# Dense products allowed beside the attention one round sooner

## The chip, the cores and the metric

The kernel runs on one core of a Trainium2 chip. The metric is the device time of one execution in microseconds (us). Three runs of the kernel before took 573.58, 574.50 and 574.53 us, with a median of 574.5 us.

## The reference

Three stages follow one another on 1536 tokens (2 batches of 768) with 512 features, all in float32:

```python
# attention: 8 heads of 64, causal window of 96 keys and 8 global keys, linear bias by distance
scores = scale * q @ k.T + bias            # masked outside the window and the global keys
x = softmax(scores) @ v                    # heads side by side: x is 1536 x 512
# first block: three products, elementwise maximum, one product
x = maximum(maximum(x @ w1, x @ w2), x @ w3) @ w_out          # 512 -> 768 -> 512
# second block: root mean square norm, gate and value, one product
xn = x / sqrt(mean(x * x) + 1e-6) * rms_g
out = (silu(xn @ w_gate) * (xn @ w_val)) @ w_out              # 512 -> 1536 -> 512
```

The weights and keys arrive as 64-bit floats, and the kernel converts the weights itself.

## The kernel before, in words

**Rounds of attention.** `FastAttention.steps` walks over 24 pieces of attention: 6 chunks of 256 tokens times 4 pairs of heads. It is a software pipeline over rounds, counted by `r` in `fast`, from 0 to 27. Round r does the scores of piece r (TensorE, L785), their maximum with bias on VectorE (L798) and their exponentials on ScalarE (L802), for the two blocks i = 0 and 1 of the chunk. In the same round it divides the piece r - 1 by its sums (`normalise`: two small VectorE operations at L810 and L811, then four GpSimd operations at L816), transposes piece r - 2 (L826, copied out at L833 and L835), multiplies piece r - 3 with the values (L849) and writes its result as a high part (ScalarE, L862). The low part of piece r - 4 is written by VectorE at L860, among the first operations of the round. The generator stops three times in a round: after the first block of exponentials (part 0), after the value products (part 1), and at the end (part 2).

**Dense products beside it.** In parts 0 and 1 of a round, `fast` may issue half a dense product of the first block: `next(side)` advances `early()`, which goes through `first(f, c)` for f = 0, 1 and the token groups c = 0, 1, 2 of 384 tokens. A dense product is 12 matmuls (L379): 4 slices of 128 features times 3 combinations of high and low parts, and its first matmul takes the low part of the weights. Its first half reads the features of the pairs 0 and 1, its second half those of the pairs 2 and 3. Six products (12 halves) make one group, so a group takes 6 rounds at two halves a round. A result is taken out of PSUM one product later, by ScalarE (L394) for the first of three weights and by VectorE (L396) for the other two. Group c may begin at the round that the condition in `fast` names: 12, 16 and 24 for c = 0, 1, 2. As each group takes 6 rounds, the groups run in the rounds 12 to 17, 18 to 23 and 24 to 27, and the last four halves of group 2 come after the attention, ahead of all other dense products, in one unbroken stretch of TensorE work.

**Weights.** `Weights.run` is a generator that converts one unit (128 x 512 weights) after another in small steps, in a cycle of four steps a unit once the ring is in use. One cycle for the unit u: a step without work; a step in which VectorE masks bits of unit u + 1 (L143) and ScalarE casts the high part of unit u (L165); a step with the second bit operation of unit u + 1 (VectorE, L145) and the scaling of unit u + 2 (ScalarE, L137); and a step with the third bit operation of unit u + 1 (VectorE, L151), the fetch of unit u + 3 and the low part of unit u (GpSimd, L168). Only then is unit u done. The steps are pushed in two ways. `pace(n)` makes n steps at the end of a round: 1 from round 1, 2 from round 8, 3 from round 12. And `need`, called by `first` ahead of each product, makes as many steps on the spot as the unit still lacks:

```python
    def need(self, key):
        while key not in self.done:
            next(self.run)
```

In group 0 a round uses one unit: the units 0 to 5 are those of (f, w) = (0, 0) to (1, 2).

**Order.** Up to the end of the attention the order of instructions on TensorE, VectorE, ScalarE and GpSimd is the order of this program (`manual(FRONT)`); the queue of DMAs on SyncE is ordered by a planner. After the attention only TensorE's order is written out, and the planner places the rest.

Of the kernel before, what the change touches and what calls it, by code (L numbers as in the profile page):

```python
# [26 lines left out]
NPAIR = H // 2  # L27
# [7 lines left out]
CN = CB * P  # L35
KC = NPREV + CB * (NG + P)
C2 = 384
NC2 = NT // C2
# [12 lines left out]
LEAD = 3  # L51
# [936 lines left out]
def program(ctx, tc, io):  # L988
# [33 lines left out]
    ngf, nlf = full[:, 0:1], full[:, 1:2]  # L1022

    fast(tc, io, (ident, gcol, mhalf), nlf, ngf)
    rv = nc.values_load(cni[0:1, 0:1], min_val=0, max_val=4)
    with tc.If(rv < 4):
# [3 lines left out]
def fast(tc, io, consts, nlf, ngf):  # L1030
    chunks = [(b, c) for b in range(B) for c in range(NCH)]

    def manual(engines):
        return tc.manual_schedule(engines={getattr(mybir.EngineType, e) for e in engines})

    with ExitStack() as ctx:
        body = Body(tc, ctx, io, consts)
        w = body.weights

        def early():  # L1040


            for c in range(NC2 - 1):
                yield from body.firsts(0, 2, c, c + 1)

        with ExitStack() as c2:
            body.warm_up(c2)
            with manual(FRONT):
                att = FastAttention(body, c2, Masks(tc, c2, nlf, ngf), chunks)
                side, n_side, r = early(), 0, 0  # L1050
                for part in att.steps():
                    if part < 2:

                        c = n_side // 12
                        if r < WARMR:
                            body.keep_warm(r)
                        if c < NC2 - 1 and r >= LEAD + 1 + NPAIR * -(-(c + 1) * C2 // CN):
                            next(side)
                            n_side += 1
                    else:  # L1060
                        if r >= WROUND:
                            w.pace(1 + (r >= WMORE) + (r >= WMOST))
                        r += 1
        body.open_behind()
        with manual(BEHIND):
            for n, _ in enumerate(side):
                w.pace(n % 2)
            for n, _ in enumerate(body.firsts(0, 2, NC2 - 1, NC2)):
                w.pace(n % 2)
            body.behind()  # L1070
            with manual(FRONT):
                body.gated()
# [77 lines left out]
```

## Time and profile before

| what | value |
| --- | --- |
| median of 3 runs | 574.5 us |
| the profiled execution | 575.12 us |
| its span, first to last instruction | 573.3 us |
| TensorE (PE) busy | 561.1 us, 98% of the span |
| VectorE (DVE) busy | 380.2 us, 66% |
| ScalarE (ACT) busy | 251.1 us, 44% |
| GpSimd (POOL) busy | 241.5 us, 42% |
| mean granted TensorE clock | 0.992 |

The profiled execution took 575.12 us, 1.82 us more than its span and 0.62 us more than the median of the runs. Busy time is an average over stages. The chain of work that ended last lies on PE for 93% of the span, so PE's order and PE's waits set the time; in the attention rounds the other engines are busy too, and what matters there is which of them is late for PE.

### The profile page before, as it was taken

To read this page: it belongs to the slowest core of one execution; us is meant where nothing else is said; L and a number is where in the kernel's file an instruction comes from. 1 tells how busy PE (TensorE), PEld (TensorE's weight loads), DVE (VectorE), ACT (ScalarE), POOL (GpSimd) and SP (SyncE) were. 2 spreads that over 40 slices of the span, in tenths; PEclk is the share of its full clock that TensorE was granted. 3 is DMA by queue.
4 is the path that set the end of the run, shared out by engine and by line. 5 is a ranking of instruction groups with operands and counts; after the bars stand their busy time and mean duration, and the time that the engine had idled before them with its cause. 6 is when DMAs were issued, how large, how long until landed. Compare 5 with 4: busy or idle time off the path is not lost.

```text
span 573.3 us, 9229 instructions
## 1 busy us (share of the span) xinstructions
PE 561.1 (98%) x3316; PEld 508.4 (89%) x3316; DVE 380.2 (66%) x801; ACT 251.1 (44%) x606; POOL 241.5 (42%) x301
## 2 busy tenths in 40 slices
PE   6999999999999999999999999999999999999995
PEld 3777888899999999988899999999999998888884
DVE  5899889628679512166778788888887879852220
ACT  3888776514244101166755444444443436442210
POOL 4555564406155001057646666555655616420000
PEclk8899999999999999999999999999999999999999
DMA  8567663202535300000000222222222104303001
GB/s 296 186 197 241 215 213 93 94 1 74 160 99 183 111 1 0 1 1 1 1 0 1 73 75 74 75 73 74 74 74 74 44 31 148 110 3 128 35 22 42
DMA packets 15895, 48.73 MB, mean 85 GB/s; under 512 B 2016, under 2 KB 2016, under 8 KB 15840
## 3 DMA queue, kind: packets, MB, share of 16 engines
q1 hardware_dynamic: 15840, 48.05, 25.9%
q8 instruction: 28, 0.46, 0.3%
q14 instruction: 27, 0.22, 0.1%
HBM read 44.90 MB, written 3.15 MB: 84 GB/s over the span
## 4 chain that ended last, share of the span: by engine, by line
PE 93%; DVE 3%; ACT 1%; POOL 1%; DMA 1%; issue 1%; SPq 0%; DVEq 0%; ACTq 0%
PE q L500 28%; PE mm L379 27%; PE acc L584 17%; PE mo L426 8%; PE sc L785 4%; PE tr L826 4%; PE av L849 4%; PE tr L460 1%; DMA ni<-nn 1%; DVE s L798 1%; PE idle L369 0%; POOL op L254 0%; ACT xb L464 0%; ACT s L802 0%; DVE z L481 0%
## 5 line engine op out<-in xcount | busy, mean ns | idle before, releaser
L500 PE MATMUL q<-xb,op 128*128 128x384 f32 x1008 | 175.5, 334 | 0.5 <-POOL op L254 0.5
L500 PEld LDWEIGHTS q<-xb,op 128*128 128x128 f32 x1008 | 174.6, 188 | 0.8 <-POOL op L254 0.8
L379 PE MATMUL mm<-xt,w 128*128 128x384 f32 x864 | 157.8, 338 | 0.0
L379 PEld LDWEIGHTS mm<-xt,w 128*128 128x128 f32 x864 | 148.4, 188 | 3.0 <-issue 2.6
L168 POOL TENSOR_TENSOR w<-x,w 128x512 fp32r<-128x512 f32 x36 | 51.8, 1442 | 82.8 <-ACT w L165 82.8
L254 POOL TENSOR_TENSOR op<-s,op 128x256 fp32r<-128x256 f32 x48 | 36.2, 766 | 57.5 <-ACT op L253 57.5
L816 POOL TENSOR_SCALAR s<-s,rs 128x232 f32<-128x232 f32 (+1 forms) x96 | 43.3, 471 | 37.0 <-DVE rs L811 27.8
L396 DVE TENSOR_TENSOR h<-mm,h 128x384 f32<-128x384 f32 x48 | 26.5, 553 | 45.8 <-PE mm L379 45.6
L426 PE MATMUL mo<-w,rst 128*128 128x512 f32 x216 | 52.1, 395 | 0.0
L802 ACT ACTIVATE s<-s,nmx 128x232 f32<-128x232 f32 (+1 forms) x96 | 44.5, 467 | 11.9 <-DVE nmx L798 11.6
L584 PE MATMUL acc<-w,gst 128*128 128x512 f32 x216 | 49.2, 389 | 0.0
L584 PE MATMUL acc<-w,st 128*128 128x512 f32 x216 | 49.1, 389 | 0.0
L584 PEld LDWEIGHTS acc<-w,st 128*128 128x128 f32 x216 | 40.5, 188 | 8.4
L584 PEld LDWEIGHTS acc<-w,gst 128*128 128x128 f32 x216 | 40.5, 188 | 8.4
L426 PEld LDWEIGHTS mo<-w,rst 128*128 128x128 f32 x216 | 39.8, 188 | 8.0
L517 DVE TENSOR_TENSOR h<-q,h 128x768 f32<-128x768 f32 (+1 forms) x39 | 34.7, 891 | 3.9 <-PE q L500 3.4
L253 ACT CAST op<-s 128x256 fp32r<-128x256 f32 x48 | 18.1, 401 | 42.2 <-DVE s L234 29.5
L798 DVE CUSTOM_DVE_ANT_0 s<-sc,bias 128x232 f32<-128x232 f32 (+1 forms) x96 | 32.0, 376 | 6.5 <-PE sc L785 4.9
L520 ACT ACTIVATE g<-g 128x768 f32<-128x768 f32 (+1 forms) x26 | 20.8, 799 | 34.0 <-DVE g L517 34.0
L165 ACT CAST w<-x 128x512 fp32r<-128x512 f32 x36 | 22.2, 619 | 26.3 <-DVE x L151 18.0
L785 PE MATMUL sc<-qk 64*128 64x232 f32 (+1 forms) x192 | 28.0, 387 | 4.2 <-DVE nmx L798 2.8
L517 DVE TENSOR_TENSOR g<-q,h 128x768 f32<-128x768 f32 (+1 forms) x13 | 11.6, 895 | 26.9 <-PE q L500 26.9
(104 smaller groups left out, 740.1 us busy)
## 6 DMA issues: line engine op xcount, KB each, us to landing
raw<-wgv SPq DMA_DIRECT2D x24, 512.0 KB, 3.6
raw<-w SPq DMA_DIRECT2D x18, 512.0 KB, 3.9
raw<-wo SPq DMA_DIRECT2D x18, 512.0 KB, 3.7
qk<-qk SPq DMA_DIRECT2D x24, 312.0 KB, 4.2
v<-vwin SPq DMA_DIRECT2D x10, 512.0 KB, 5.6
out<-o SPq DMA_DIRECT2D x12, 256.0 KB, 2.1
v<-vwin SPq DMA_DIRECT2D x2, 256.0 KB, 5.4
gcol<-gcol SPq DMA_DIRECT2D x1, 2.0 KB, 1.6
```

Of the source, the lines that this page charges most:

```text
L168: self.nc.gpsimd.tensor_tensor(out=t[:, 1, :], in0=self.x.pop(i), in1=t[:, 0, :], op=ALU.subtract)
L254: nc.gpsimd.tensor_tensor(out=t[:, 1, :], in0=s, in1=t[:, 0, :], op=ALU.subtract)
L379: self.nc.tensor.matmul(ps, w[:, wi, k * P:(k + 1) * P], x[b][:, k, xi, c0:c0 + C2], start=(i == 0), stop=(i == 3 * KT - 1),)
L396: self.nc.vector.tensor_tensor(out=h, in0=ps, in1=h, op=ALU.max)
L426: self.nc.tensor.matmul(ps, h[:, k % 3, hi, :], w[:, wi, :], start=(k + x == 0), stop=(k == NF1 - 1 and x == 2),)
L500: nc.tensor.matmul(ps, a[:, wi, k * P:(k + 1) * P], self.xb[b][:, j, k, xi, :], start=(i == 0), stop=(i == 5))
L517: nc.vector.tensor_tensor(out=o, in0=ps, in1=x, op=ALU.add)
L584: self.nc.tensor.matmul(ps, of(si), w[:, wi, :], start=(f == LAST[0] and si == 1), stop=(f == LAST[-1] and si == 0 and wi == 0),)
L785: nc.tensor.matmul(sc[j][:, i, :n], qk[r, i * P:(i + 1) * P], qk[r, k0:k0 + n], start=True, stop=True)
L798: nc.vector.tensor_tensor_reduce(out=s[:, j, :n], in0=self.sc[d][j][:, i, :n], in1=self.bias(n, 2 * pr + j), scale=-QK, scalar=3.0e38, op0 ...
L802: nc.scalar.activation(s[:, j, :n], s[:, j, :n], AF.Exp, bias=nmx[:, j:j + 1], scale=-1.0, accum_out=sm[:, i, j:j + 1])
L816: nc.gpsimd.tensor_scalar(s[:, j, :n], s[:, j, :n], rs[:, i, j:j + 1], 1.0, op0=ALU.mult, op1=ALU.mult)
```

## The change

The constant in the condition is one smaller. Group c may begin at the rounds 11, 15 and 23 in place of 12, 16 and 24. Nothing else differs; the steps of `pace` stay tied to the round's number.

```diff
                         c = n_side // 12
                         if r < WARMR:
                             body.keep_warm(r)
-                        if c < NC2 - 1 and r >= LEAD + 1 + NPAIR * -(-(c + 1) * C2 // CN):
+                        if c < NC2 - 1 and r >= LEAD + NPAIR * -(-(c + 1) * C2 // CN):
                             next(side)
                             n_side += 1
```

## Rows read from the trace of the kernel before

**Rows 1.** Page, part 1: busy time, share of the span and instructions of each engine.

```profile
PE 561.1 (98%) x3316; PEld 508.4 (89%) x3316; DVE 380.2 (66%) x801; ACT 251.1 (44%) x606; POOL 241.5 (42%) x301
```

**Rows 2.** Page, part 5: busy us, mean ns | idle us before.

```profile
L379 PE MATMUL mm<-xt,w 128*128 128x384 f32 x864 | 157.8, 338 | 0.0
```

**Rows 3.** Windows by round, 11 to 16: length, busy us by engine, clock, DMA.

```profile
42.40:45.94 3.54, 3.42 (x33) 2.69 (x33) 3.47 (x15) 3.54 (x12) 1.77 (x5) 1.00 0.86 315
45.94:51.42 5.48, 5.48 (x45) 4.49 (x45) 5.41 (x18) 4.58 (x20) 3.65 (x7) 1.00 0.72 235
51.42:56.58 5.16, 5.16 (x46) 4.19 (x45) 5.06 (x16) 3.80 (x13) 3.26 (x5) 1.00 0.71 228
56.58:61.52 4.94, 4.94 (x43) 3.98 (x42) 4.70 (x19) 4.37 (x14) 2.84 (x5) 1.00 0.39 86
61.52:66.25 4.73, 4.73 (x40) 3.76 (x39) 3.86 (x16) 3.04 (x11) 2.85 (x5) 1.00 0.90 334
66.25:71.14 4.89, 4.89 (x39) 3.92 (x38) 3.96 (x15) 3.38 (x13) 1.59 (x4) 1.00 0.70 219
```

**Rows 4.** Chain in order of time, after the attention: start us, us, what.

```profile
118.68 67.80 PE mm L379 x390
```

**Rows 5.** Timeline of PE, rounds 11 to 16: start us, us, what.

```profile
43.70 1.09 PE L826 MATMUL tr<-ident,s 128*128 128x128 f32 x8
44.72 1.10 PE L849 MATMUL av<-at,v 104*64 104x128 f32 x16
...
47.07 1.09 PE L826 MATMUL tr<-ident,s 128*128 128x128 f32 x8
...
49.14 1.10 PE L849 MATMUL av<-at,v 104*64 104x128 f32 x16
50.17 1.31 PE L379 MATMUL mm<-xt,w 128*128 128x384 f32 x6
...
58.02 1.30 PE L379 MATMUL mm<-xt,w 128*128 128x384 f32 x6
...
62.97 1.29 PE L379 MATMUL mm<-xt,w 128*128 128x384 f32 x6
...
67.86 1.29 PE L379 MATMUL mm<-xt,w 128*128 128x384 f32 x6
```

**Rows 6.** Timeline of POOL, rounds 12 to 21.

```profile
51.89 1.66 POOL L168 TENSOR_TENSOR w<-x,w 128x512 fp32r<-128x512 f32 x1 [1.27 <-ACT w L165]
...
57.31 1.59 POOL L816 TENSOR_SCALAR s<-s,rs 128x128 f32<-128x128 f32 x4 [1.73 <-ACT w L165]
58.87 1.28 POOL L168 TENSOR_TENSOR w<-x,w 128x512 fp32r<-128x512 f32 x1
...
71.27 1.28 POOL L168 TENSOR_TENSOR w<-x,w 128x512 fp32r<-128x512 f32 x1 [3.21 <-ACT w L165]
...
93.50 3.20 POOL L816 TENSOR_SCALAR s<-s,rs 128x232 f32<-128x232 f32 x4 [0.44 <-PE tr L826]
```

**Rows 7.** Timeline of DVE, rounds 12 to 14, and one row of round 21.

```profile
51.72 0.69 DVE L151 SCALAR_TENSOR_TENSOR x<-raw,x 128x512 int32<-128x512 int32 x1
...
55.68 0.42 DVE L143 TENSOR_SCALAR x<-x 128x512 int32<-128x512 int32 x1
...
56.74 0.17 DVE L810 TENSOR_SCALAR rs<-sm 128x4 f32<-128x4 f32 x1
...
57.60 0.29 DVE L798 CUSTOM_DVE_ANT_0 s<-sc,bias 128x128 f32<-128x128 f32 x1 [0.17 <-PE sc L785]
...
58.03 0.55 DVE L396 TENSOR_TENSOR h<-mm,h 128x384 f32<-128x384 f32 x1
...
59.13 0.69 DVE L835 COPY at<-tr 128x512 f32<-128x512 f32 x1
59.73 0.97 DVE L151 SCALAR_TENSOR_TENSOR x<-raw,x 128x512 int32<-128x512 int32 x1
...
93.53 0.95 DVE L143 TENSOR_SCALAR x<-x 128x512 int32<-128x512 int32 x2
```

## The prediction

> **What bounds the kernel now.** I read the page first: PE is busy for 561.1 us, 98% of the span [rows 1], and of the 864 dense matmuls of the first block none had idle time ahead of it [rows 2]. So only two things can change the time: work taken off PE's queue where it is the bound, or a new wait on PE. Next the windows, one for each round [rows 3]: a round with two dense halves lasts 4.73 to 5.48 us and PE is busy throughout; round 11, the last without them, lasts 3.54 us, and there VectorE (3.47) and ScalarE (3.54) are as full as PE (3.42). The chain of waits shows what comes after the attention: one piece of 390 dense matmuls in 67.80 us without a gap [rows 4], 0.174 us each. Last the timelines of PE, GpSimd and VectorE around rounds 11 to 16 [rows 5 to 7], for how early each weight unit is ready.
>
> **The move on PE.** Every group slides by one round: group 0 to rounds 11 to 16, group 1 to 17 to 22, group 2 to 23 to 27. Rounds 12 to 27 keep two halves each, round 11 gains two, and two halves leave the stretch after the attention.
>
> What leaves: 12 x 0.174 = 2.09 us.
>
> What round 11 gains: between transposes and values the first half adds (49.14 - 47.07) - (44.72 - 43.70) = 1.05 us; values take 50.17 - 49.14 = 1.03; from the second half to the next round's scores it is 51.42 - 50.17 = 1.25 [rows 3, 5]. Values of round 11 began at 44.72, so round 12 begins at 44.72 + 1.05 + 1.03 + 1.25 = 48.05 in place of 45.94. Round 12 no longer waits for VectorE to clear the scores, so it costs what round 13 does, 5.16 in place of 5.48. Round 13 begins at 53.21 in place of 51.42: 1.79 later. The move alone is worth 1.79 - 2.09 = -0.30 us: round 11 was already nearly full, so little was free there.
>
> The inputs of round 11 cost nothing: its first half reads pieces 0, 1, 4, 5, finished two rounds before; its second half needs piece 7's low part, which VectorE writes at the round's start, ahead of that round's maxima, and PE comes to it only after transposes, a half and values (3.1 us). If that cover failed it would cost up to the 0.4 us of one such operation. The evacuations move with their products; VectorE's round 12 chain stays short enough, since its first result goes to ScalarE.
>
> **The weights.** Counting steps in the code, unit u is done with step 10 + 4u. By the end of round 10 `pace` has made 13 steps, by the ends of rounds 11 to 15 it has made 15, 18, 21, then 25 and 29 once a forced step is added in each of rounds 14 and 15. Unit u is now needed in round 11 + u. Units 0 to 2 (steps 10, 14, 18) are done in time; units 3, 4, 5 (22, 26, 30) each lack exactly one step, so `need` makes it on the spot in rounds 14, 15, 16. That step holds GpSimd's low part, which the product's first matmul reads, and an L151 on VectorE between the two blocks' maxima. Before, 12 + u left each unit done at the end of the previous round; even so unit 5's low part ended at 71.27 + 1.28 = 72.55 in round 17, which began at 71.14 and came to its dense half some 1.6 us later: 0.2 us to spare [rows 3, 5, 6].
>
> Forced or not, GpSimd takes that operation after the round's normalise (57.31, then 58.87 in round 14 [rows 6]), as before. Now PE waits for it, and behind the waiting matmul stand the values, the second half and the next scores. The wait comes out of these durations [rows 6, 7]: VectorE's first maximum 1.02 us after the round's start (57.60 - 56.58); block 0 of the maxima 0.43; evacuation and block 1 1.10 (0.55 without the evacuation); copy 0.60; L143 and L145 1.06; from the division's start to the normalise 0.57; normalise 1.56; low part 1.28. PE comes to its dense half 1.44, 1.45 and 1.61 us after the start of rounds 14, 15 and 16.
>
> Round 14, begun at 53.21 + 5.16 = 58.37: round 13's chain is 53.21 + 1.02 + 0.43 + 1.10 + 0.60 + 1.06 = 57.42 for the division, 57.99 normalise, 59.55 low part, ready at 60.83. Wanted at 59.81: PE waits **1.02**.
>
> Round 15, begun at 58.37 + 4.94 + 1.02 = 64.33: round 14's maxima of block 0 end at 59.82; the forced L151 comes while the low part runs. When that happened before, L151 took 0.97 and ended 0.55 after the low part [rows 6, 7]; so it ends at 61.38; + 1.10 + 0.60 + 1.06 = 64.14 for the division, normalise 64.71 to 66.27, ready 67.55. Wanted 65.78: PE waits **1.77**.
>
> Round 16, begun at 64.33 + 4.73 + 1.77 = 70.83: round 15's L151 begins at 65.78 and takes its undisturbed 0.69 [rows 7]; + 0.55 + 0.60 + 1.06 = 68.68, normalise 69.25 to 70.81, ready 72.09. Wanted 72.44: **no wait**; the earlier wait gave the other engines time.
>
> Sum: -0.30 + 1.02 + 1.77 = +2.49 us. Bounds: if L151 never waited for GpSimd, round 15's wait is 0.90 and round 16's 0.52, in all -0.30 + 1.02 + 0.90 + 0.52 = +2.14. If round 15's L151 waits too, to 67.55 + 0.55, round 16 waits 1.28: +3.77. If the low parts were ready, -0.30. I take +2.49, from the rows nearest to it. Unit 2 ended at 51.89 + 1.66 = 53.55 [rows 6] and is wanted near 54.65 in round 13: no wait, and 1 us of slack if ScalarE's cast slips behind the later values.
>
> Row 58.87 with row 59.73 shows that L151 and the low part exclude each other. A normalise took 3.20 us beside two L143 [rows 6, 7], against 1.59 (smaller tiles) in round 14, so it takes part too. The Trainium skill (SBUF — State Buffer, section "SBUF: two separate sides") states it as an exclusive lock: a VectorE operation with two SBUF inputs or in a two-port mode and a GpSimd operation block each other for a whole instruction. By it round 15's L151 and the normalise would push each other, the low part would be ready at about 68.24, the wait there 2.46 and none in round 16: an estimate of +3.18 us in place of +2.49.
>
> Rounds 17 on need no new weights until after the attention, and PE is their bound, so the 2.49 us are not won back. The profiled execution would take 575.12 + 2.5 = 577.6; its 0.62 us over the median are its own, so the median goes from 574.5 to **577.0**.
>
> **Rivals.**
> *No wait, not slower:* the low parts of units 3 to 5 come before PE does, at the dense half's place in rounds 14 to 16. Then only the move is left, 574.2. It decides at 1 us: the normalise of round 14 would have to start at 56.97 in place of 57.99. For it: no dense matmul waited before [rows 2]. Against: the normalise hangs on the division behind the previous round's maxima, and PE's round 14 is not later relative to those than before.
> *The waits repeat:* L151 loses to GpSimd in rounds 14 and 15 and PE waits in all three rounds, +3.8, 578.3. For it: the 0.97 and the 3.20. By the lock as the skill states it the waits would be longer without repeating; its 577.7 lies between this and the forecast and shares this chance. Against: after each long wait the next round's chain starts from a late PE, which takes from its wait.
> *The planner's part:* after the attention VectorE and ScalarE work is placed anew, and VectorE already runs later units' L143 in round 21 [rows 7]. If these moves freed or delayed PE by 1 us, the time would be 576 or 578; PE's 67.80 us without a gap [rows 4] speak against it.
> That the change does nothing is out: r = 11 satisfies the new condition.
>
> **Chances.** The forecast with the bounds around it 0.60, repeated waits 0.15, no wait 0.15, a planner's move 0.10. From no change this kernel can be told at about 0.2%, 1.15 us. The forecast and repeated waits are slower, with a little of the forecast's low side and half of the planner's case within the bound: slower 0.76; no wait falls mostly within it: same 0.18; faster 0.06. The range reaches from the no-wait case's edge, 574.4, to 579.0, repeated waits with 0.7 more.
>
> **What would show it.** Dense matmuls from round 11, at about 45 us. In the list of waits a new row of PE's L379 waiting for POOL's L168, two or three times, some 2 to 4 us in all; L151 once or twice near 1.5 us in these rounds. Round 13 begins near 53.2, the last values near 118.7 + 1.8 + 2.8 = 123, and the unbroken stretch after them is 2.1 us shorter. Wrong if L379 waits for nothing, or if the wait sits at another place.

## The result, and the profile after

The changed kernel took 577.88 us (median of 4 runs, 576.88 to 578.92) against 574.11 us for the kernel before (573.58 to 574.53): a ratio of 1.0063, 95% interval 1.0048 to 1.0079. It is slower by 3.8 us. The forecast was slower by 2.5 us. Here and below the ratio and its interval come from the undisturbed runs alone (two of the twelve of experiment 3 were disturbed, at 620 and 1115 us). The ratio is not the quotient of the two medians; the two can differ by 0.001.

The profiled execution took 576.88 us, its span 575.0 us. The list of PE's waits has one row that the kernel before did not have, the second one here (the kernel before had no idle time ahead of any L379 [rows 2]). Columns: engine and line, what it waited for, us in total, times, longest us.

```profile
PE sc L785 <- DVE nmx L798: 3.1, 5, 1.1
PE mm L379 <- POOL w L168: 2.8, 2, 2.0
```

The windows by round answer to [rows 3]: the rounds 11 to 16, each from the start of its scores to the start of the next. The columns are the length; the busy us (and instructions) of PE, of its weight loads, of VectorE, ScalarE and GpSimd; the granted clock; the DMA share and GB/s.

```profile
41.43:47.08 5.65, 5.65 (x45) 4.66 (x45) 5.58 (x18) 5.32 (x19) 3.65 (x7) 1.00 0.90 322
47.08:52.24 5.16, 5.16 (x45) 4.20 (x44) 4.93 (x19) 3.60 (x13) 1.82 (x5) 1.00 0.61 177
52.24:57.40 5.16, 5.16 (x45) 4.20 (x44) 3.83 (x16) 3.86 (x13) 3.15 (x7) 1.00 0.54 165
57.40:63.42 6.02, 5.22 (x44) 4.02 (x43) 4.92 (x16) 3.66 (x13) 2.44 (x5) 1.00 0.53 139
63.42:70.36 6.94, 4.99 (x40) 3.79 (x39) 4.66 (x17) 3.93 (x14) 5.11 (x10) 1.00 0.79 276
70.36:75.25 4.89, 4.89 (x39) 3.93 (x39) 3.77 (x13) 3.31 (x12) 1.11 (x1) 1.00 0.39 116
```

Round 11 now holds two dense halves and lasts 5.65 us. Round 14 lasts 6.02 us in place of 4.94, round 15 6.94 in place of 4.73, and in just these two PE is busy for less than the round. Round 16 lasts what it lasted. PE's timeline shows where the holes are; the bracket is the idle time ahead of the row and what ended it. They answer to the dense halves of [rows 5].

```profile
43.58 1.29 PE L379 MATMUL mm<-xt,w 128*128 128x384 f32 x6
...
59.90 1.32 PE L379 MATMUL mm<-xt,w 128*128 128x384 f32 x6 [0.80 <-POOL w L168]
...
67.06 1.31 PE L379 MATMUL mm<-xt,w 128*128 128x384 f32 x6 [1.95 <-POOL w L168]
```

The brackets count from the end that the profile models for the transposes. Counted by starts, the dense halves begin 59.90 - 57.40 = 2.50 and 67.06 - 63.42 = 3.64 us after the start of their rounds, in place of 1.44 and 1.45: 1.06 and 2.19 us later, nearly all that the two rounds grew by.

The timelines of GpSimd and of VectorE in the rounds 14 and 15 answer to [rows 6, 7].

```profile
57.03 1.58 POOL L816 TENSOR_SCALAR s<-s,rs 128x128 f32<-128x128 f32 x4 [2.01 <-DVE rs L811]
58.58 1.26 POOL L168 TENSOR_TENSOR w<-x,w 128x512 fp32r<-128x512 f32 x1
63.64 2.13 POOL L816 TENSOR_SCALAR s<-s,rs 128x128 f32<-128x128 f32 x4 [3.80 <-DVE rs L811]
65.74 1.26 POOL L168 TENSOR_TENSOR w<-x,w 128x512 fp32r<-128x512 f32 x1
```

```profile
58.86 1.53 DVE L151 SCALAR_TENSOR_TENSOR x<-raw,x 128x512 int32<-128x512 int32 x1
...
63.07 0.16 DVE L810 TENSOR_SCALAR rs<-sm 128x4 f32<-128x4 f32 x1
...
64.76 0.69 DVE L151 SCALAR_TENSOR_TENSOR x<-raw,x 128x512 int32<-128x512 int32 x1
```

The low part ends at 59.84 and at 67.00, and each time PE's dense half begins 0.06 us later. The chain in order of time gives the start of the unbroken dense stretch after the attention, [rows 4]:

```profile
122.73 77.33 PE mm L379 x445
```

Up to round 11 both kernels run the same program, and its length differs from execution to execution: between 12 and 20 us the granted clock was 0.50 and then 0.72 (4 us each) in the profile of before, 0.59 and then 1.00 in this one. So I count from the start of round 11's scores: 122.73 - 41.43 = 81.30 us to the stretch, where it was 118.68 - 42.40 = 76.28. From the stretch's start to the end of the span it is 575.0 - 122.73 = 452.27 in place of 573.3 - 118.68 = 454.62. So the trace accounts for 5.02 - 2.35 = +2.67 us, while the medians differ by 3.77. That gap of 1.1 us was the open question for the experiments.

### The profile page after: what moved, and what is told of

It reads as the page before. It is cut to its first block, busy times and chain, and to the rows that moved or that the text cites. A ratio compares the mean times of both kernels' runs of the same rounds, so it can differ in the third digit from the quotient of the medians.

```text
span 575.0 us, 9225 instructions
## 1 busy us (share of the span) xinstructions
PE 560.1 (97%) x3316; PEld 507.5 (88%) x3316; DVE 380.4 (66%) x801; ACT 251.4 (44%) x606; POOL 240.1 (42%) x301
## 3 DMA queue, kind: packets, MB, share of 16 engines
HBM read 44.90 MB, written 3.15 MB: 84 GB/s over the span
## 4 chain that ended last, share of the span: by engine, by line
PE 92%; DVE 4%; POOL 1%; issue 1%; DMA 1%; ACT 1%; SPq 0%; DVEq 0%; ACTq 0%; POOLq 0%
PE q L500 28%; PE mm L379 26%; PE acc L584 17%; PE mo L426 8%; PE sc L785 4%; PE tr L826 4%; PE av L849 4%; PE tr L460 1%; DVE s L798 1%; DMA qk<-qk 1%; PE idle L369 0%; POOL op L254 0%; ACT xb L464 0%; POOL s L816 0%; DVE z L481 0%
## 5 line engine op out<-in xcount | busy, mean ns | idle before, releaser
L379 PE MATMUL mm<-xt,w 128*128 128x384 f32 x864 | 158.1, 338 | 2.8 <-POOL w L168 2.8
L379 PEld LDWEIGHTS mm<-xt,w 128*128 128x128 f32 x864 | 148.4, 188 | 6.0 <-POOL w L168 3.2
```

What stands on the lines that cost most here:

```text
L379: self.nc.tensor.matmul(ps, w[:, wi, k * P:(k + 1) * P], x[b][:, k, xi, c0:c0 + C2], start=(i == 0), stop=(i == 3 * KT - 1),)
```

## The experiments

Ratios are to the kernel before, run beside each kernel on the same chip (573.72 us in the first four experiments, 573.78 us in the next four).

**1. The changed kernel again.**

> The changed kernel itself, once more, beside the kernel before. Theory (PE waits for the low parts of the weight units 3 to 5): again two or three waits of PE's dense matmuls (L379) for GpSimd's L168 in rounds 14 to 16, lengthening these rounds by 3.0 to 3.6 us in all; from the start of round 11's scores to the start of the unbroken dense stretch 81.0 to 81.6 us against 76.3 before; ratio to before 1.004 to 1.006. Rival (most of the loss comes from outside these rounds, since the timed runs differ by 3.8 us and the profiles from round 11 on by only 2.7): a ratio of 1.006 or more with waits of 3.3 us, and in the profile a second place, later than round 16, that is over 1 us slower than before.

577.91 us, ratio 1.0068 (1.0049 to 1.0087). The waits were as before, 2.6 us in two, but 123.77 - 41.09 = 82.68 us passed from round 11 to the stretch, 1.4 more than in the first profile. All of it lies in round 15, which lasted 71.44 - 63.09 = 8.35 us. PE's timeline there:

```profile
66.61 1.64 PE L379 MATMUL mm<-xt,w 128*128 128x384 f32 x6 [1.82 <-POOL w L168]
68.17 1.55 PE L849 MATMUL av<-at,v 128*64 128x128 f32 x12
69.65 1.85 PE L379 MATMUL mm<-xt,w 128*128 128x384 f32 x6
71.44 1.05 PE L785 MATMUL sc<-qk 64*128 64x232 f32 x8
```

The same 12 value matmuls take 0.88 us in other rounds. The windows show what differs (the number after the engines' busy times is the granted TensorE clock):

```profile
66.61:67.30 0.69, 0.69 (x4) 0.69 (x5) 0.66 (x3) 0.29 (x2) 0.00 (x0) 1.00 0.82 260
67.30:70.90 3.60, 3.60 (x20) 2.83 (x19) 1.11 (x4) 1.13 (x3) 1.74 (x5) 0.53 0.51 198
70.90:71.44 0.54, 0.54 (x4) 0.29 (x3) 0.00 (x0) 0.33 (x1) 0.54 (x1) 1.00 0.00 0
```

In the 3.6 us from 0.69 us after the second wait on, the granted clock was 0.53 in the mean, about the lower of its two levels, 1.2 and 2.4 GHz. In the first profile it was 1.00 there. Neither theory nor rival had this: the second loss is in the same round as the wait, not later.

**2. Conversion sooner, from the early rounds.**

```diff
-WMORE = 8
+WMORE = 5
```

> The changed kernel with the second conversion step a round from round 5 on in place of round 8 (WMORE = 5): three steps earlier, so that no unit needs a forced step. Theory: the dense waits for L168 fall from 3.3 us to under 0.4 us, the rounds 14, 15, 16 last 4.9, 4.7 and 4.9 us, and the time is 0.3 us (up to 0.6) below the kernel before, ratio 0.9985 to 1.0005, if the three added steps hide in rounds 5 to 7; each that does not costs up to 0.7 us. Rival (the loss is the planner's or the moved halves' own, not the weights'): still 1.004 or more.

576.61 us, ratio 1.0046 (1.0030 to 1.0061). No dense matmul waited for GpSimd any more, and from round 11 to the stretch it was 122.44 - 44.33 = 78.11 us, 3.2 less than in the first profile of the changed kernel. The waits are gone as the theory said, yet the time is where the rival put it, and the reason is a third one: the three added steps did not hide. The rounds 4 to 10 took 24.97 us:

```profile
19.36:44.33 24.97, 22.66 (x220) 17.14 (x219) 23.58 (x92) 20.93 (x74) 13.98 (x29) 1.00 0.53 167
```

Before, they took 42.40 - 19.65 = 22.75 us, with VectorE busy for 20.79 of them, 91%; now it is 23.58 us, 94%. In these rounds PE's scores waited 2.3 us for VectorE, against 0.6 before. Over the whole execution it is 4.6 us, against 2.8:

```profile
PE sc L785 <- DVE nmx L798: 4.6, 6, 1.3
```

The three added steps cost 24.97 - 22.75 = 2.22 us, about the 0.7 us a step that I had named as the most. The medians differ by 2.9 us; the rest is not placed.

**3. The low part of the weights last in each product.**

```diff
-        for k in range(KT):
-            for wi, xi in ((1, 0), (0, 1), (0, 0)):
+        order = [(k, 0, xi) for k in range(KT) for xi in (1, 0)] + [(k, 1, 0) for k in range(KT)]
+        for k, wi, xi in order:
...
-            if k == KT // 2 - 1:
+            if i == 6:
                 yield
```

> The changed kernel with another order in each dense product: the eight matmuls with the high part of the weights first, the four with the low part last, so that the first half needs no low part. The forced steps stay where they are. Theory (PE's wait for the low part is the loss): the wait moves to the last two thirds of the second half, some 2.8 us later, and vanishes but for 0.3 us; ratio 0.9985 to 1.001. Rival (the forced step's VectorE work between the maxima is the loss, by making the next scores late): rounds 14 and 15 stay 1 us or more longer than before, ratio 1.003 or more.

Ratio 1.0010 (0.9995 to 1.0024). The forced steps are still there; only PE's need for the low part comes later. Round 14 lasts 63.36 - 58.41 = 4.95 us, as before the change; round 15 lasts 5.55, with one wait inside the second half:

```profile
68.02 0.96 PE L379 MATMUL mm<-xt,w 128*128 128x384 f32 x4 [0.55 <-POOL w L168]
```

The theory holds in place and kind; I had expected at most 0.3 us to be left and 0.55 was. In round 14, which also has a forced L151 between the maxima (59.87 to 61.44), PE lost nothing, so that work by itself does not delay PE in its round.

**4. The kernel before with late weights.** No dense product is moved.

```diff
-WMORE = 8
-WMOST = 12
+WMORE = 10
+WMOST = 13
```

> The kernel before, dense products from round 12 as there, but conversion made one round later (WMORE = 10, WMOST = 13), so that the units 3, 4 and 5 are forced in rounds 15, 16 and 17 just as the changed kernel forces them in 14, 15 and 16. Theory (the weights alone are the loss): waits of L379 for L168 of 2 to 3.6 us in these rounds, and with 0.3 us less VectorE work ahead of round 12 a ratio of 1.003 to 1.006, as for the changed kernel. Rival (it takes the earlier dense products to make the loss): within 0.002 of the kernel before.

577.87 us, ratio 1.0071 (1.0050 to 1.0093): a loss as large as the changed kernel's, without the change. One row of the list of waits, and two windows of the round with the second wait:

```profile
PE mm L379 <- POOL w L168: 2.9, 2, 1.9
```

```profile
65.91:69.60 3.69, 1.86 (x15) 1.32 (x14) 3.13 (x13) 2.58 (x10) 3.25 (x5) 1.00 0.35 101
...
70.90:74.48 3.58, 3.58 (x20) 2.81 (x19) 0.60 (x2) 1.46 (x3) 2.90 (x5) 0.53 0.11 42
```

The ratio is above the 1.006 that I gave for the waits alone, and the fall of the clock is here too: 0.53 behind a wait of 1.89 us.

**5. The forced steps made one round end earlier.**

```diff
-                            w.pace(1 + (r >= WMORE) + (r >= WMOST))
+                            w.pace(1 + (r >= WMORE) + (r >= WMOST) + (13 <= r <= 15))
```

> The changed kernel with one conversion step more at the end of each of rounds 13, 14 and 15 (four in place of three), so that the steps that were forced inside the next rounds are made at the end of the rounds before, ahead of the next normalise on GpSimd. Theory (only the lateness of the low parts costs): L379's waits for L168 fall to under 0.4 us, no fall of the granted clock after round 11, 78.0 to 78.6 us from round 11's scores to the unbroken dense stretch (82.7 in the first experiment, 76.3 before), ratio to before 0.999 to 1.001. Rival (the same number of steps in rounds 13 to 15 loads VectorE as much as the forced steps did, and the scores become late instead): ratio 1.003 or more, with waits of the scores for VectorE in rounds 14 to 17.

573.72 us, ratio 1.0005 (0.9995 to 1.0015): in three rounds one step is made at the end of the round before and not inside the round, and the loss is gone. The rounds 13 to 16 make 15 steps as in the changed kernel, the forced ones counted, so the amount of VectorE's work was not the cause. GpSimd now does the low part ahead of the normalise:

```profile
56.97 1.27 POOL L168 TENSOR_TENSOR w<-x,w 128x512 fp32r<-128x512 f32 x1 [2.23 <-ACT w L165]
58.21 1.58 POOL L816 TENSOR_SCALAR s<-s,rs 128x128 f32<-128x128 f32 x4
61.91 1.36 POOL L168 TENSOR_TENSOR w<-x,w 128x512 fp32r<-128x512 f32 x1 [2.12 <-ACT w L165]
63.71 1.58 POOL L816 TENSOR_SCALAR s<-s,rs 128x128 f32<-128x128 f32 x4 [0.44 <-DVE rs L811]
```

In round 14 (57.12 to 62.06) the low part is ready at 58.24, where in the changed kernel PE waited for it until 2.5 us into the round. The rounds 14 and 15 last 4.94 and 4.73 us, the clock stays at 1.00, and 119.34 - 41.15 = 78.19 us pass to the stretch.

```profile
57.12:62.06 4.94, 4.94 (x43) 3.98 (x42) 4.32 (x15) 3.54 (x13) 2.82 (x6) 1.00 0.72 193
62.06:66.79 4.73, 4.73 (x39) 3.76 (x38) 4.63 (x16) 3.43 (x13) 2.80 (x5) 1.00 0.86 298
```

**6. Experiments 3 and 5 together.**

> The extra step at the end of rounds 13 to 15 and the product order with the low part of the weights last, together on the changed kernel. Theory: no wait of a dense matmul for GpSimd at all, so that what is left is the move alone: 78.0 to 78.2 us from round 11's scores to the unbroken stretch, ratio 0.999 to 1.000. Rival (half of the measured gain of the product order came from something else): ratio 1.001 or more.

573.76 us, ratio 0.9997 (0.9986 to 1.0008), 120.39 - 42.29 = 78.10 us to the stretch and 572.5 - 120.39 = 452.11 behind its start, no wait for GpSimd. This is the move alone, and by its time it cannot be told from no change.

**7. Control: the product order of experiment 3 on the kernel before.**

> Control: the kernel before with the product order that has the low part of the weights last. Theory: no dense matmul waited before, so nothing changes, ratio 0.999 to 1.001, and 76.2 to 76.4 us from round 11's scores to the unbroken stretch. Rival (the order itself slows or speeds the products): the stretch after the attention differs by more than 0.5 us.

573.70 us, ratio 1.0000 (0.9990 to 1.0010), 118.29 - 41.98 = 76.31 us to the stretch and 572.4 - 118.29 = 454.11 us behind its start. The order by itself does nothing, so what it gave in experiment 3 came from the wait. The traces of experiments 6 and 7 have the same product order and no wait, and differ by the move alone: 78.10 - 76.31 = 1.79 us more up to the stretch and 454.11 - 452.11 = 2.00 less behind its start, -0.21 in all.

**8. Both dense halves behind the values.**

```diff
                     if part < 2:
-                        c = n_side // 12
                         if r < WARMR:
                             body.keep_warm(r)
-                        if c < NC2 - 1 and r >= LEAD + NPAIR * -(-(c + 1) * C2 // CN):
-                            next(side)
-                            n_side += 1
+                        for _ in range(2 * part):
+                            c = n_side // 12
+                            if c < NC2 - 1 and r >= LEAD + NPAIR * -(-(c + 1) * C2 // CN):
+                                next(side)
+                                n_side += 1
```

> The changed kernel with both dense halves of a round after the value products in place of one on either side of them; the forced steps come after the copy then. PE reaches the first low part 1 us later, so theory expects the waits to fall by up to 1 us each, to 0 to 0.3 us in round 14 and 1.0 to 1.6 us in round 15; and, if the fall of the clock that the first and fourth experiments showed after the wait of 1.8 to 1.9 us comes from PE's pause, a granted clock of 1.00 through round 15; ratio 1.001 to 1.004. Rival (the clock falls for another reason, as of the load on the chip): a stretch at about 0.5 in rounds 14 to 16 here too.

574.85 us, ratio 1.0009 (0.9998 to 1.0021). Round 14 has no wait, round 15 one of 0.8 us, a little under the 1.0 to 1.6 expected, and the clock was 1.00. Rows of GpSimd, VectorE and PE in round 15:

```profile
63.67 1.59 POOL L816 TENSOR_SCALAR s<-s,rs 128x128 f32<-128x128 f32 x4 [2.95 <-DVE rs L811]
65.23 1.27 POOL L168 TENSOR_TENSOR w<-x,w 128x512 fp32r<-128x512 f32 x1
...
65.82 1.23 DVE L151 SCALAR_TENSOR_TENSOR x<-raw,x 128x512 int32<-128x512 int32 x1
...
66.55 2.38 PE L379 MATMUL mm<-xt,w 128*128 128x384 f32 x12 [0.82 <-POOL w L168]
```

Work that PE can do in the meantime takes most of the loss away. Not all of it is that: the forced L151 comes later too, behind the normalise (63.67 to 65.26), and the low part is ready 66.50 - 63.23 = 3.27 us after the round's start in place of 67.00 - 63.42 = 3.58. With the pause short the clock stayed; one profile does not prove that it always would.

**9 and 10. Two more profiles of the changed kernel,** for how often the clock falls.

> The changed kernel, one more profile, for how often the granted clock falls after the long wait. Theory (the fall belongs to the usual execution and makes the difference between the 2.7 us of the first profile and the 4.1 us of the timed runs): a stretch near half the clock behind the wait of round 15, which lasts 8.2 to 8.6 us, and 82.4 to 83.0 us from round 11's scores to the unbroken dense stretch. Rival (the first profile was the usual one): round 15 in 6.9 to 7.0 us at a clock of 1.00, and 81.3 us.

> The same once more: round 15 of 8.2 to 8.6 us with the fall of the clock, if that is the usual case; 6.9 to 7.0 us if not.

One of each, on the same chip. Experiment 9 took 578.95 us, with 125.01 - 42.17 = 82.84 us from round 11 to the stretch. Its second wait, and the window in which round 15 ended:

```profile
67.81 1.32 PE L379 MATMUL mm<-xt,w 128*128 128x384 f32 x6 [1.96 <-POOL w L168]
```

```profile
67.81:72.68 4.87, 4.87 (x25) 3.90 (x25) 1.61 (x5) 1.64 (x5) 2.67 (x5) 0.65 0.55 201
```

Experiment 10 took 577.38 us, with 123.47 - 42.32 = 81.15 us to the stretch, and has these two:

```profile
67.83 1.31 PE L379 MATMUL mm<-xt,w 128*128 128x384 f32 x6 [1.80 <-POOL w L168]
```

```profile
67.83:71.13 3.30, 3.30 (x25) 2.63 (x25) 1.77 (x6) 1.44 (x5) 1.69 (x5) 1.00 0.56 200
```

The same 25 matmuls take 4.87 us at a mean clock of 0.65 and 3.30 us at 1.00. Of four profiles of the changed kernel two show the fall; four are too few to say how often it comes.

## Why the prediction was right, and where its size was off

The direction and the mechanism held; the size was short by 1.3 us of 3.8 in the first timing (2.5 against 3.8) and by 1.7 in the second (577.91 - 573.72 = 4.19).

**The move:** forecast 1.79 us later at round 13; measured (52.24 - 41.43) - (51.42 - 42.40) = 1.79. What leaves the end was forecast as 2.09; the stretch and all behind it shortened by 2.35 against the profile of before, and by 1.84 against the control (454.11 - 452.27). Experiments 6 and 7, with no wait in either, give -0.21. So the -0.30 is right within what executions differ by, and the time of experiment 6, the move alone, says that it is too small to measure. Round 11 was full, as argued.

**The lateness of units 3 to 5:** right, by exactly the counted steps. Experiments 3, 4 and 5 show it from three sides: PE's need moved later, the lateness without the move, the move without the lateness.

**Round 14:** forecast a wait of 1.02; the round grew by 6.02 - 4.94 = 1.08.

**Round 15:** forecast 1.77; it grew by 6.94 - 4.73 = 2.21. The chain was right up to the division, forecast 64.14 - 58.37 = 5.77 us after round 14's start and measured 63.07 - 57.40 = 5.67, and so was L151 in round 14, which ended 0.55 us behind the low part (58.86 + 1.53 against 58.58 + 1.26). The term that was mis-sized is the normalise of round 15: 2.13 us in place of 1.56, because L151 ran in it from 64.76 on. From the start of the normalise to the end of the low part it is 67.00 - 63.64 = 3.36 us, where the sum had 1.56 + 1.28 = 2.84. I had set the delay between normalise and L151 aside for the sum. With the lock that the Trainium skill states (SBUF — State Buffer, section "SBUF: two separate sides") the prediction's estimate was 2.46; the round's growth lies between the two, 0.25 short of that estimate. Experiment 8 separates the two operations: there L151 began after the normalise, which took 1.59, and the low part ended 66.50 - 63.67 = 2.83 us after the normalise began. In experiment 1 L151 met them otherwise:

```profile
63.30 1.58 POOL L816 TENSOR_SCALAR s<-s,rs 128x128 f32<-128x128 f32 x4 [3.80 <-DVE rs L811]
64.86 1.70 POOL L168 TENSOR_TENSOR w<-x,w 128x512 fp32r<-128x512 f32 x1
...
64.44 0.99 DVE L151 SCALAR_TENSOR_TENSOR x<-raw,x 128x512 int32<-128x512 int32 x1
```

The normalise kept its 1.58, the low part took 1.70 in place of 1.28, and the two together 3.26; experiment 10 is like it with 3.25, experiment 9 like the first profile with 3.36. So an L151 that falls on them costs 0.4 to 0.5 us either way. Whether the two engines exclude each other or merely slow each other is not decided by any run here. The row of 3.20 us in the prediction showed less than it was taken for: it is of larger tiles, which took 1.77 us elsewhere in the same trace and not 1.59, and VectorE ran L145 beside it as well as the two L143.

**Round 16:** forecast no wait; measured none, 4.89 us in both.

**What was missing:** the clock. The prediction had no term for what PE's pauses do to the granted clock. In two of four profiles it fell behind the second wait. Set beside the profile with the same wait and no fall, that cost 8.51 - 6.94 = 1.57 us (experiment 9 and the first profile, waits of 1.96 and 1.95) and 8.35 - 6.80 = 1.55 us (experiments 1 and 10, 1.82 and 1.80). Without a fall, from round 11 on, the changed kernel's first profile is 2.67 us longer than the profile of before. That profile's end is itself long: behind the stretch's start it has 454.62 us, where experiments 4 and 7, with the same work there, both have 454.11. Against experiment 7 the first profile is (81.30 - 76.31) - (454.11 - 452.27) = 3.15 us longer. So the trace gives 2.7 to 3.2 us without the fall and 4.2 to 4.7 with it, and the differences of the medians, 3.77 and 4.19, lie between.

Which of the timed executions had the fall is not shown, but the mean granted clock of each is on record. It is 0.991 and 0.989 in the two profiles with the fall, 0.994 and 0.993 in the two without; eight of the ten executions of the changed kernel in the first timing and experiment 1 have 0.991 or less. Executions of the kernel before reach 0.991 too, at up to 575.93 us, so a low mean alone does not prove the fall. That it makes most of the gap is likely, not shown.

**The rivals:** "no wait" fell with the two waits. "The waits repeat" fell too, since round 16 had none, though its 578.3 was nearer to the medians (577.88 and 577.91) than the forecast's 577.0: it has no term for the clock either, so that is luck. The prediction's other estimate, +3.18 us with the delay between normalise and L151 counted in, came close to the 3.15 of the trace without a fall, in part by luck: the wait of round 15 was 0.25 shorter than in it, and 1.84 us left the end in place of 2.09. The planner's part is not seen: the stretch after the attention changed by what left it, within 0.3 us.

## What to carry to other kernels

When work is moved earlier, count again when each of its inputs is produced, in the steps of whatever paces the producer: here the tokens were ready and three weight units were one conversion step late each, which lengthened two rounds by 3.3 us where the move could win 0.3. A helper that makes up a missing step on the spot hides such lateness, since nothing breaks and only the time shows it; making the step at the end of the round before took the loss away. And before spending idle time of one engine, look at the others: adding three steps to rounds in which VectorE was already 91% busy cost 2.2 us.

## What the hardware showed that was not expected

A wait of TensorE can cost more than its length. Behind waits of 0.82 and 1.82 us, the dense halves that ended them 7 us apart, the granted clock fell from 1.00 to 0.53 for 3.6 us (experiment 1), and behind 1.02 and 1.89 us in the same way (experiment 4). Behind waits of 0.80 and 1.95 us it stayed at 1.00 in the first profile of the changed kernel, and behind 0.81 and 1.96 us it fell in experiment 9, so the length of the waits alone does not settle it. What does is open.

A few hundredths of a microsecond went with which of two GpSimd operations was delayed. In all four profiles of the changed kernel VectorE's L151 begins in the normalise of round 15. Where it began 1.11 or 1.12 us after the normalise's start (experiment 9 and the first profile), L151 took 0.69 and the normalise 2.13 us; where it began 1.14 or 1.15 us after it (experiments 1 and 10), L151 took 0.99 and 0.97, the normalise 1.58 and the low part behind it 1.70.
